# First weight loads moved between the attention jobs, transposes moved ahead of their predecessor's last part, and the second norm moved among the first unit's groups

## Chip, cores, metric

One core of one Trainium2 chip. The metric is the device time of one execution in microseconds (us), lower is better. Engines: PE is TensorE, DVE is VectorE, ACT is ScalarE, POOL is GpSimd, SP is SyncE. "Lnnn" is a line of the kernel that the lines belong to; the kernel after has its lines up to 8 lower down than the kernel before (L264 became L269, L470 became L477, and so on).

## The reference

```python
q, k, v: (8 batches, 8 heads, 576, 64) float32
scores = q @ k^T / 8                            # per batch and head
ret = scores * where(i >= j, gamma_h ** (i - j), 0)
attn = ret @ v                                  # (8, 8, 576, 64)
x = attn.transpose(0, 2, 1, 3).reshape(4608, 512)
xn = x / sqrt(mean(x * x) + 1e-6) * rms_g
out = (silu(xn @ w_gate) * (xn @ w_val)) @ w_out    # 512 -> 1536 -> 512
```

The three weight matrices come as float64 (their random parts are multiplied by a NumPy scalar of 64 bits), and the kernel makes float32 of them on the chip.

## The kernel before

The attention is cut into 32 jobs, one for a batch and a pair of heads. A job is five pieces of work: `turn` (q and k turned over by PE; later jobs use `prepare`, the same on DVE), `scores` and `states` (PE), `weigh` (DVE: the mask, and the running state), `values` and `carried` (PE: the product with v, and what the earlier chunks of tokens add). `carried` ends with three DVE multiplications that write the job's part of x. Four jobs give a batch's 576 tokens.

The FFN goes by units of 384 tokens, so jobs 0 to 3 feed the first unit and jobs 4 to 7 the second. Units 0 and 1 are done plainly, in 12 groups of 32 matmuls (`up_plain(u, m, g)`: unit, gate or value, third of the columns); from unit 2 on a Strassen scheme is used, which the change does not touch.

What matters for this change is what shares the engines with the first 226 us:

```python
    def slot(j, rest=True):             # the order on PE and DVE
        if j < len(jobs):
            scores(j)
            states(j)
        if rest and j > 0:
            values(j - 1)
        if j < len(jobs):
            weigh(j)
        if rest and j > 0:
            carried(j - 1)

    def weigh(j):
        ret = d["ret"] = att.tile([P, 2, NFULL * P], F32, tag="ret", ..., bufs=1)   # one copy only
        ...
    def weights_to(n):                  # conversion of the 18 chunks of 1 MB
        while n_chunks < min(n, len(chunks)):
            mantissa(n_chunks + 1)      # 3 DVE operations
            join(n_chunks)              # 1 DVE operation: the chunk is ready
            load_chunks(n_chunks + 4)   # 1 MB, one DMA
            exponent(n_chunks + 2)      # 1 DVE operation, then 3 ACT passes
            n_chunks += 1

    # start():
        for j in range(NHP):                        # NHP = 4
            load_first(j)                           # q, k of a job, issued by SP
            if j + 1 < NHP:
                load_kv(j)                          # v of a job, issued by SP
        for i in (2, 3, 0, 1, 4):
            table(i)                                # issued by ACT
        load_chunks(2)                              # issued by ACT
        table(5)
        ...
        load_chunks(3)
        turn(0)                                     # its results are copied by ACT
        for j in range(NHP):
            slot(j)
            if j + 1 < NHP:
                turn(j + 1)
            ...                                     # squares, conversion of chunks 0 and 1
        ...                                         # last part of job 3, first norm
        order = [(0, 0, 0), 4, (0, 1, 0), 5, (0, 0, 1), 6, (0, 1, 1), 7, (0, 0, 2)]
        order += [(1, 0, 0), (1, 1, 0), (0, 1, 2)]
        order += [(1, m, g) for g in (1, 2) for m in range(2)]
        for what in order:
            if not isinstance(what, tuple):
                slot(what, rest=what > NHP)         # a job
                following(what)
                if what == 2 * NHP - 1:
                    values(what); carried(what); norm_0(1); norm_1(1)
                continue
            u, m, g = what
            weights_to(4 * g + 2 * m + 2)
            for _ in up_plain(u, m, g):             # 4 steps of 8 matmuls
                step += 1
                weights_to(2 + (step + 1) // 2)     # one chunk every two steps
            if what == (0, 0, 2):
                norm_2(1)
```

Of the kernel before, what the change touches and what calls it, by code (L numbers as in the profile page):

```python
# [10 lines left out]
F32 = mybir.dt.float32  # L11
# [32 lines left out]
def kernel(  # L44
# [32 lines left out]

    const = ctx.enter_context(tc.tile_pool(name="const", bufs=1))
    raw = ctx.enter_context(tc.tile_pool(name="raw", bufs=1))
    att = ctx.enter_context(tc.tile_pool(name="att", bufs=2))  # L80
    xp = ctx.enter_context(tc.tile_pool(name="xp", bufs=3))
    ffn = ctx.enter_context(tc.tile_pool(name="ffn", bufs=1))
    tmp = ctx.enter_context(tc.tile_pool(name="tmp", bufs=6))
# [4 lines left out]
    def bank(name):  # L88
        return banks.tile([P, 512], F32, tag="b", name=name)
# [57 lines left out]
    def load_first(j):  # L147


        b, hp = jobs[j]  # L150
        part = h_of[0].rearrange("p f t -> p (f t)")[:, j * 6 * P : j * 6 * P + 6 * P]
        part = part.rearrange("p (c e d) -> p c e d", e=2, d=D)
        t = raw.tile([P, NFULL, 2, D], F32, tag="k", name=f"k_{j}", bufs=4)
        st[j].update(q=part[:, :NFULL], qt=part[:TAIL, NFULL], k=t, kt=part[:TAIL, NFULL + 1])
        for nm, src in (("q", q), ("k", k)):
            for e in range(2):
                nc.sync.dma_start(
                    out=st[j][nm][:, :, e],
                    in_=src[b, 2 * hp + e, : NFULL * P].rearrange("(c p) d -> p c d", p=P),
                )  # L160
            nc.sync.dma_start(
                out=st[j][nm + "t"],
                in_=src[b, 2 * hp : 2 * hp + 2, NFULL * P :].rearrange("e p d -> p e d"),
            )

    def load_kv(j):


        b, hp = jobs[j]
        for nm, src, bufs in (("k", k, 4), ("v", v, 3)):  # L170
            if nm in st[j]:
                continue
            t = raw.tile([P, NFULL, 2, D], F32, tag=nm, name=f"{nm}_{j}", bufs=bufs)
            for e in range(2):
                nc.sync.dma_start(
                    out=t[:, :, e],
                    in_=src[b, 2 * hp + e, : NFULL * P].rearrange("(c p) d -> p c d", p=P),
                )
            st[j][nm] = t
        t = st[j]["vt"] = raw.tile([P, D], F32, tag="vt", name=f"vt_{j}", bufs=3)  # L180
        for e in range(2):
            nc.sync.dma_start(
                out=t[e * TAIL : e * TAIL + TAIL], in_=v[b, 2 * hp + e, NFULL * P :]
            )

    def turn(j):

        d = st[j]
        last = bank(f"turn_{j}_t")
        for i, nm in enumerate("qk"):  # L190
            ps = bank(f"turn_{j}_{nm}")
            for c in range(NFULL):
                nc.tensor.transpose(
                    out=ps[:, c * P : c * P + P], in_=d[nm][:, c].rearrange("p e d -> p (e d)"),
                    identity=ident,
                )
            o = slice(i * TAIL, i * TAIL + TAIL)
            nc.tensor.transpose(
                out=last[:, o], in_=d[nm + "t"].rearrange("p e d -> p (e d)"),
                identity=ident[:TAIL, :TAIL],  # L200
            )
            t = d[nm + "T"] = att.tile([P, S], F32, tag=nm + "T", name=f"{nm}T_{j}")
            nc.scalar.copy(out=t[:, : NFULL * P], in_=ps)
            nc.scalar.copy(out=t[:, NFULL * P :], in_=last[:, o])
        scale_v(j)

    def prepare(j):
# [39 lines left out]
    def states(j):  # L247

        d = st[j]
        for c in range(NFULL):  # L250
            for e in range(2):
                nc.tensor.matmul(  # L252
                    d["s"][e * D : e * D + D, 2, SC + c * D : SC + c * D + D],
                    lhsT=d["k"][:, c, e], rhs=d["v"][:, c, e], start=True, stop=True,
                )
# [62 lines left out]
            )  # L318
        st[j] = {}

    def slot(j, rest=True):

        if j > len(jobs):
            return
        if j < len(jobs):
            scores(j)
            states(j)
        if rest and j > 0:
            values(j - 1)
        if j < len(jobs):  # L330
# [3 lines that stand above are left out]
# [179 lines left out]

        return i % 4 if i < n_up else LATER[i - n_up]

    def load_chunk(i):
        dst, src, rws, cols = chunks[i]
        if src.dtype != F32:
            n = dst.shape[1]
            cols = slice(2 * (cols.start or 0), 2 * cols.stop if cols.stop else None)  # L520
            src = src.bitcast(U32)
            at = spare(i)
            dst = free[:, : 4 * DM] if at == 3 else (
                w_out[:, 4 * at : 4 * at + 4].rearrange("p c f -> p (c f)")
            )
            dst = words_of[i] = dst.bitcast(U32).rearrange("p (c f) -> p c f", c=n)
            waits_at[at] = i
        nc.scalar.dma_start(out=dst, in_=src[rws, cols].rearrange("(c p) f -> p c f", p=P))

    def load_chunks(n):  # L530

        nonlocal n_loads
        while n_loads < min(n, len(chunks)) and waits_at.get(spare(n_loads)) is None:
            load_chunk(n_loads)
            n_loads += 1

    def exponent(i):
# [58 lines left out]
    def weights_to(n):  # L596

        nonlocal n_chunks
        while n_chunks < min(n, len(chunks)):
            mantissa(n_chunks + 1)  # L600
            join(n_chunks)
            load_chunks(n_chunks + 4)
            exponent(n_chunks + 2)
            n_chunks += 1
# [3 lines left out]
    def start():  # L608

        h_of[0] = ffn.tile([P, NF, U], F32, tag="h", name="h_0")  # L610
        tables = [*_causal_tables(), *_decay_tables(H, D)]
        tables = list(zip((causal, causal_t, gv, gt, gc, gq), tables))

        def table(i):
            t, values_ = tables[i]
            src = nc.inline_tensor(values_, name=t.tensor.name + "_table")
            nc.scalar.dma_start(out=t, in_=src.ap())

        make_identity(nc, ident)
        for t in sd:  # L620
            nc.gpsimd.memset(t, 0.0)
        nc.vector.memset(ones, 1.0)
        for j in range(NHP):
            load_first(j)
            if j + 1 < NHP:
                load_kv(j)
        for i in (2, 3, 0, 1, 4):
            table(i)
        load_chunks(2)
        table(5)  # L630
        nc.scalar.dma_start(out=rms_g, in_=moe_rms_g.rearrange("(c p) -> p c", p=P))
        load_chunks(3)
        turn(0)
        sq = []
        for j in range(NHP):
            slot(j)
            if j + 1 < NHP:
                turn(j + 1)
            if j:
                sq.append(square(0, j - 1))  # L640
            if j == 0:
                exponent(0)
                exponent(1)
            elif j == 1:
                load_kv(NHP - 1)
                mantissa(0)
                weights_to(1)
                load_qk(NHP)
            elif j == 2:
                weights_to(2)  # L650
                load_kv(NHP)
        values(NHP - 1)
        carried(NHP - 1)
        sq.append(square(0, NHP - 1))
        norm_0(0, sq)
        norm_1(0)
        norm_2(0)
        following(NHP - 1)
        step = 0
        order = [(0, 0, 0), 4, (0, 1, 0), 5, (0, 0, 1), 6, (0, 1, 1), 7, (0, 0, 2)]  # L660
        order += [(1, 0, 0), (1, 1, 0), (0, 1, 2)]
        order += [(1, m, g) for g in (1, 2) for m in range(2)]
        for what in order:
            if not isinstance(what, tuple):
                slot(what, rest=what > NHP)
                following(what)
                if what == 2 * NHP - 1:
                    values(what)
                    carried(what)
                    norm_0(1)  # L670
                    norm_1(1)
                continue
            u, m, g = what
            weights_to(4 * g + 2 * m + 2)
            for _ in up_plain(u, m, g):
                step += 1
                weights_to(2 + (step + 1) // 2)
            if what == (0, 0, 2):
                norm_2(1)
        weights_to(len(chunks))  # L680
        combine(0)
        for u in (1, 0):
            for s in range(NS):
                down(u, s)
                if u == 0:
                    (norm_0, norm_1, norm_2)[s](2)
            if u:
                combine(1)
                slot(8, rest=False)
                following(8)  # L690
        slot(9)
        following(9)
# [51 lines left out]
```

## Time and profile before

| | kernel before |
|---|---|
| median | 1265.76 us |
| span of the profiled run | 1264.4 us |
| PE busy | 1217.4 us (96%), so 47.0 us idle |
| mean granted PE clock | 0.984 |
| first gate group of unit 0 | 65.47 us |
| first group of unit 1 | 153.39 us |
| last plain group ends (the next product starts) | 225.7 us |

The timeline: start, duration, engine, line, operation, output from input; the bracket is idle time before the instruction and what ended it.

### The profile page before, as it was taken

The page shows a single profiled execution, that of the slowest core. Times are in us where ns is not written, and L with a number is a line of the kernel's source. Part 1 is how long each engine was busy: PE and PEld are TensorE (multiplying, and loading weights), DVE is VectorE, ACT ScalarE, POOL GpSimd, SP SyncE. Part 2 cuts the span into 40 slices and gives each one's busy share as a digit, 9 for nine tenths or more (in the row PEclk, how much of TensorE's full clock was granted, in tenths as well). Part 3 has the DMA queues.
Part 4 walks back from the last instruction along what each step waited for, and adds up shares of the span by engine and source line. Part 5 has one row for each costly group of instructions (what it writes and reads, how often), then busy time and mean ns, then how long its engine had stood idle before and what let it go on. Part 6 is the DMA issues. An engine that isn't in the chain of part 4 may idle for free.

```text
span 1264.4 us, 16414 instructions
## 1 busy us (share of the span) xinstructions
PE 1217.4 (96%) x6792; PEld 924.2 (73%) x6792; DVE 547.6 (43%) x1056; ACT 280.3 (22%) x520; POOL 43.0 (3%) x44
## 2 busy tenths in 40 slices
PE   4599799999999999999999999999999999999998
PEld 3465455447976985976985995995995896795993
DVE  1789871015542652433552464343454443333240
ACT  3646541011221220111120221121221121120110
POOL 0000005130000000000000000000000000000000
PEclk8899799999999999999999999999999999999999
DMA  8579520022230322002122233002122200000000
GB/s 212 123 177 198 141 100 0 17 62 45 46 74 17 68 51 54 1 9 54 38 40 58 38 59 68 9 1 53 27 57 53 45 1 10 17 1 17 9 1 25
DMA packets 225307, 65.68 MB, mean 52 GB/s; under 512 B 212688, under 2 KB 212816, under 8 KB 225232
## 3 DMA queue, kind: packets, MB, share of 16 engines
q1 hardware_dynamic: 215872, 45.12, 17.3%
q10 hardware_dynamic: 9360, 19.51, 4.7%
q8 instruction: 53, 0.87, 0.3%
q14 instruction: 22, 0.18, 0.0%
HBM read 55.16 MB, written 9.44 MB: 51 GB/s over the span
## 4 chain that ended last, share of the span: by engine, by line
PE 88%; DVE 5%; ACT 3%; DMA 2%; issue 1%; SPq 1%; POOL 0%; DVEq 0%; ACTq 0%; POOLq 0%
PE out L484 29%; PE x L413 12%; PE w L413 12%; PE z L413 12%; PE y L413 6%; PE up L470 6%; PE s L242 3%; PE av L292 2%; PE av L306 2%; PE s L252 1%; DMA k<-in_k_dram 1%; ACT w_gate L548 1%; PE ms L360 1%; DVE w_gate L572 1%; DMA v<-in_v_dram 1%
## 5 line engine op out<-in xcount | busy, mean ns | idle before, releaser
L484 PE MATMUL out<-w_out,h 128*128 128x512 f32 x792 | 346.1, 594 | 0.0
L484 PEld LDWEIGHTS out<-w_out,h 128*128 128x128 f32 x792 | 149.1, 190 | 177.5 <-issue 175.1
L489 ACT COPY o_all<-out 128x512 f32<-128x512 f32 x36 | 21.1, 586 | 348.8 <-PE out L484 334.9
L420 DVE TENSOR_TENSOR u<-m,y 128x384 f32<-128x384 f32 x60 | 33.2, 554 | 149.9 <-PE y L413 141.8
L264 DVE TENSOR_TENSOR ret<-s,causal 128x1024 f32<-128x1024 f32 x32 | 39.2, 1224 | 121.8 <-PE av L292 69.3
L413 PE MATMUL x<-x,w_gate 128*128 128x192 f32 x480 | 88.9, 328 | 1.5 <-ACT m L437 1.5
L413 PE MATMUL x<-x,w_val 128*128 128x192 f32 x480 | 89.2, 329 | 0.0
L413 PE MATMUL w<-sums,w_gate 128*128 128x192 f32 x480 | 87.8, 326 | 0.0
L413 PE MATMUL w<-sums,w_val 128*128 128x192 f32 x480 | 87.8, 326 | 0.0
L413 PE MATMUL z<-x,w_gate 128*128 128x192 f32 x480 | 87.8, 326 | 0.0
L413 PE MATMUL z<-x,w_val 128*128 128x192 f32 x480 | 87.8, 326 | 0.0
L413 PEld LDWEIGHTS x<-x,w_gate 128*128 128x128 f32 x480 | 79.2, 190 | 7.1 <-issue 4.3
L413 PEld LDWEIGHTS x<-x,w_val 128*128 128x128 f32 x480 | 78.8, 190 | 1.4 <-ACT m L437 1.4
L413 PEld LDWEIGHTS w<-sums,w_gate 128*128 128x128 f32 x480 | 79.7, 190 | 0.0
L413 PEld LDWEIGHTS z<-x,w_val 128*128 128x128 f32 x480 | 79.7, 190 | 0.0
L413 PEld LDWEIGHTS z<-x,w_gate 128*128 128x128 f32 x480 | 79.7, 190 | 0.0
L413 PEld LDWEIGHTS w<-sums,w_val 128*128 128x128 f32 x480 | 79.7, 190 | 0.0
L280 ACT ACTIVATE sd<-sum,gc 64x256 f32<-64x256 f32 x64 | 32.3, 504 | 200.4 <-DVE sum L274 200.0
L470 PE MATMUL up<-x,w_gate 128*128 128x384 f32 x192 | 67.8, 515 | 1.5 <-ACT w_gate L548 0.8
L420 DVE TENSOR_TENSOR h<-u,w 128x384 f32<-128x384 f32 x60 | 33.3, 555 | 81.4 <-PE w L413 81.4
L432 ACT ACTIVATE h<-h 128x384 f32<-128x384 f32 x90 | 47.0, 523 | 88.6 <-DVE h L420 88.6
L382 DVE SCALAR_TENSOR_TENSOR x<-x,rms_g,rb 128x384 f32<-128x384 f32 x48 | 26.3, 608 | 89.1 <-PE rb L380 89.1
(98 smaller groups left out, 1345.7 us busy)
## 6 DMA issues: line engine op xcount, KB each, us to landing
out_dram<-o_all SPq DMA_DIRECT2D x36, 256.0 KB, 2.0
k<-in_k_dram SPq DMA_DIRECT2D x64, 128.0 KB, 2.8
v<-in_v_dram SPq DMA_DIRECT2D x64, 128.0 KB, 2.8
qraw<-in_q_dram SPq DMA_DIRECT2D x112, 72.0 KB, 2.4
kraw<-in_k_dram SPq DMA_DIRECT2D x112, 72.0 KB, 2.6
w_out<-in_moe_w_gate_dram ACTq DMA_DIRECT2D x6, 1024.0 KB, 6.6
w_out<-in_moe_w_val_dram ACTq DMA_DIRECT2D x3, 1024.0 KB, 5.9
w_gate<-in_moe_w_val_dram ACTq DMA_DIRECT2D x3, 1024.0 KB, 6.2
```

The costliest lines, as they stand in the source:

```text
L242: nc.tensor.matmul(s[:, e, ck] if c < NFULL else s[e * n : e * n + n, 2, :n], lhsT=d["kT"][r, ck], rhs=d["qT"][r, ck], start=True, stop=True,)
L264: nc.vector.tensor_tensor(out=ret.rearrange("p e (c k) -> p e c k", c=NFULL), in0=s[:, :2].rearrange("p e (c k) -> p e c k", c=NFULL), in1 ...
L280: nc.scalar.activation(out=sd[j % 2][r, :, r], in_=t[r], func=AF.Copy, scale=gc[r, hp : hp + 1])
L292: nc.tensor.matmul(av[blk][e * D : e * D + D, o : o + n], lhsT=d["v"][:, c, e] if c < NFULL else d["vt"][r], rhs=d["ret"][:, e, c * P : c ...
L306: nc.tensor.matmul(av[blk][:, o : o + n], lhsT=sd[j % 2][:, c - 1], rhs=d["qT"][:, c * P : c * P + n], start=False, stop=(c in (AC - 1, NC ...
L382: nc.vector.scalar_tensor_tensor(out=x[:, c], in0=x[:, c], scalar=rms_g[:, c : c + 1], in1=rb[:, :U], op0=ALU.mult, op1=ALU.mult,)
L413: nc.tensor.matmul(ps[:, i * HU : i * HU + HU], lhsT=w_up[m][:, 2 * blk + c, cut], rhs=t_of[u][blk][:, c], start=(start and i == c == 0), ...
L420: nc.vector.tensor_tensor(out=o, in0=a, in1=pairs_of(ps), op=ALU.add)
L432: nc.scalar.activation(out=o, in_=c, func=AF.Silu)
L470: nc.tensor.matmul(ps[:, :U], lhsT=w_up[m][:, 4 * half + c, i * P : i * P + P], rhs=x_of[u][:, c], start=(c == 0), stop=(c == NHP - 1),)
L484: nc.tensor.matmul(ps[:, :DM], lhsT=h_of[u][:, f, s * P : s * P + P], rhs=w_out[:, f], start=(f == 0), stop=(f == NF - 1),)
L489: nc.scalar.copy(out=o, in_=ps[:, :DM])
```

## The change

The intent, in its author's words: "First chunks of weights issued by SP between the jobs; a job's transposes ahead of the last part of its predecessor; second norm among the first unit's groups". I count four parts. (1) Loads: SP issues the first three chunks, each behind a job's loads; ACT keeps the small tables. (2) Transposes: `turn(j+1)` goes ahead of `values(j-1)`, with all transposes ahead of their ACT copies and a third copy of qT and kT. (3) Conversion: one chunk less is converted before the first norm, and some of what stays is done one job later. (4) Order: all groups of unit 0 come ahead of those of unit 1, and the second norm is spread over its last two groups. The diff, cut to these:

```diff
-    att = ctx.enter_context(tc.tile_pool(name="att", bufs=2))
+    att = ctx.enter_context(tc.tile_pool(name="att", bufs=3))
 ... (the tile of k: bufs=4 -> 3; the ACT copies of turn(j) become fetch(j);
 ...  load_chunk, load_chunks and table get a queue as argument)
     def slot(j, rest=True, between=None):
         if j < len(jobs):
             scores(j)
             states(j)
+        if between is not None:
+            between(j + 1)
         if rest and j > 0:
             values(j - 1)
 ...
-        for j in range(NHP):
-            load_first(j)
-            if j + 1 < NHP:
-                load_kv(j)
         for i in (2, 3, 0, 1, 4):
             table(i)
-        load_chunks(2)
-        table(5)
         nc.scalar.dma_start(out=rms_g, ...)
-        load_chunks(3)
+        for j in range(NHP - 1):
+            load_first(j)
+            load_kv(j)
+            if j == 1:
+                table(5, nc.sync)
+            load_chunks(j + 1, nc.sync)
         turn(0)
+        fetch(0)
+        def ahead(j):
+            if j < NHP:
+                turn(j)
+                fetch(j)
         for j in range(NHP):
-            slot(j)
-            if j + 1 < NHP:
-                turn(j + 1)
+            slot(j, between=ahead)
             if j == 0:
+                load_first(NHP - 1)
                 exponent(0)
-                exponent(1)
             elif j == 1:
                 load_kv(NHP - 1)
+                load_qk(NHP)
+                exponent(1)
                 mantissa(0)
-                weights_to(1)
-                load_qk(NHP)
             elif j == 2:
-                weights_to(2)
                 load_kv(NHP)
+                weights_to(1)
 ...
-        order = [..., (0, 1, 1), 7, (0, 0, 2)]
-        order += [(1, 0, 0), (1, 1, 0), (0, 1, 2)]
-        order += [(1, m, g) for g in (1, 2) for m in range(2)]
+        order = [..., (0, 1, 1), 7, (0, 0, 2), (0, 1, 2)]
+        order += [(1, m, g) for g in range(NG) for m in range(2)]
 ...
-                if what == 2 * NHP - 1:
-                    values(what); carried(what); norm_0(1); norm_1(1)
+                if what == (0, 1, 2) and step % 4 == 2:      # inside the group
+                    norm_1(1)
             if what == (0, 0, 2):
+                values(2 * NHP - 1); carried(2 * NHP - 1); norm_0(1)
+            if what == (0, 1, 2):
                 norm_2(1)
```

More of the change, by code (lines that the diff above doesn't have):

```diff
@@ L152, in load_first @@
         part = part.rearrange("p (c e d) -> p c e d", e=2, d=D)
-        t = raw.tile([P, NFULL, 2, D], F32, tag="k", name=f"k_{j}", bufs=4)
+        t = raw.tile([P, NFULL, 2, D], F32, tag="k", name=f"k_{j}", bufs=3)
         st[j].update(q=part[:, :NFULL], qt=part[:TAIL, NFULL], k=t, kt=part[:TAIL, NFULL + 1])
@@ L169, in load_kv @@
         b, hp = jobs[j]
-        for nm, src, bufs in (("k", k, 4), ("v", v, 3)):
+        for nm, src, bufs in (("k", k, 3), ("v", v, 3)):
             if nm in st[j]:
@@ L189, in turn @@
         last = bank(f"turn_{j}_t")
+        d["turned"] = []
         for i, nm in enumerate("qk"):
@@ L201, in turn, with fetch @@
             )
-            t = d[nm + "T"] = att.tile([P, S], F32, tag=nm + "T", name=f"{nm}T_{j}")
+            d["turned"].append((nm, ps, last[:, o]))
+    def fetch(j):
+        for nm, ps, last in st[j].pop("turned"):
+            t = st[j][nm + "T"] = att.tile([P, S], F32, tag=nm + "T", name=f"{nm}T_{j}")
             nc.scalar.copy(out=t[:, : NFULL * P], in_=ps)
-            nc.scalar.copy(out=t[:, NFULL * P :], in_=last[:, o])
+            nc.scalar.copy(out=t[:, NFULL * P :], in_=last)
         scale_v(j)
@@ L319, in carried, with slot @@
         st[j] = {}
-    def slot(j, rest=True):
+    def slot(j, rest=True, between=None):
         if j > len(jobs):
@@ L514, in spare, with load_chunk @@
         return i % 4 if i < n_up else LATER[i - n_up]
-    def load_chunk(i):
+    def load_chunk(i, queue):
         dst, src, rws, cols = chunks[i]
@@ L527, in load_chunk, with load_chunks @@
             waits_at[at] = i
-        nc.scalar.dma_start(out=dst, in_=src[rws, cols].rearrange("(c p) f -> p c f", p=P))
-    def load_chunks(n):
+        queue.dma_start(out=dst, in_=src[rws, cols].rearrange("(c p) f -> p c f", p=P))
+    def load_chunks(n, queue=nc.scalar):
         nonlocal n_loads
         while n_loads < min(n, len(chunks)) and waits_at.get(spare(n_loads)) is None:
-            load_chunk(n_loads)
+            load_chunk(n_loads, queue)
             n_loads += 1
@@ L612, in start, with table @@
         tables = list(zip((causal, causal_t, gv, gt, gc, gq), tables))
-        def table(i):
+        def table(i, queue=nc.scalar):
             t, values_ = tables[i]
             src = nc.inline_tensor(values_, name=t.tensor.name + "_table")
-            nc.scalar.dma_start(out=t, in_=src.ap())
+            queue.dma_start(out=t, in_=src.ap())
         make_identity(nc, ident)
@@ L641, in start @@
             if j == 0:
+                load_first(NHP - 1)
                 exponent(0)
-                exponent(1)
             elif j == 1:
                 load_kv(NHP - 1)
+                load_qk(NHP)
+                exponent(1)
                 mantissa(0)
+            elif j == 2:
+                load_kv(NHP)
                 weights_to(1)
-                load_qk(NHP)
-            elif j == 2:
-                weights_to(2)
-                load_kv(NHP)
         values(NHP - 1)
@@ L659, in start @@
         step = 0
-        order = [(0, 0, 0), 4, (0, 1, 0), 5, (0, 0, 1), 6, (0, 1, 1), 7, (0, 0, 2)]
-        order += [(1, 0, 0), (1, 1, 0), (0, 1, 2)]
-        order += [(1, m, g) for g in (1, 2) for m in range(2)]
+        order = [(0, 0, 0), 4, (0, 1, 0), 5, (0, 0, 1), 6, (0, 1, 1), 7, (0, 0, 2), (0, 1, 2)]
+        order += [(1, m, g) for g in range(NG) for m in range(2)]
         for what in order:
@@ L666, in start @@
                 following(what)
-                if what == 2 * NHP - 1:
-                    values(what)
-                    carried(what)
-                    norm_0(1)
-                    norm_1(1)
                 continue
@@ L677, in start @@
                 weights_to(2 + (step + 1) // 2)
+                if what == (0, 1, 2) and step % 4 == 2:
+                    norm_1(1)
             if what == (0, 0, 2):
+                values(2 * NHP - 1)
+                carried(2 * NHP - 1)
+                norm_0(1)
+            if what == (0, 1, 2):
                 norm_2(1)
```

## The prediction

> **What bounds the kernel now.** I read the table of slices first, then stretches of ten microseconds, then the chain that ended last, then the timeline of the first 226 us. Busy time over the whole span says little here, since the change touches only the start.
>
> ```profile
> PE   4599799999999999999999999999999999999998
> DVE  1789871015542652433552464343454443333240
> ...
> PE 88%; DVE 5%; ACT 3%; DMA 2%; issue 1%; SPq 1%; POOL 0%; DVEq 0%; ACTq 0%; POOLq 0%
> ```
>
> A slice is 31.6 us. PE is full from the sixth slice on; what can be won lies in slices 1 to 5. VectorE is heaviest in just those.
>
> ```profile
> 0.00:10.00 10.00, 1.38 (x5) 0.90 (x5) 0.34 (x6) 0.00 (x0) 1.64 (x8) 1.00 0.79 220
> 60.00:70.00 10.00, 7.29 (x17) 4.16 (x17) 6.00 (x12) 0.75 (x1) 0.87 (x1) 0.54 0.10 16
> 110.00:120.00 10.00, 9.72 (x30) 5.43 (x30) 9.82 (x19) 5.87 (x9) 0.00 (x0) 1.00 0.92 226
> 120.00:130.00 10.00, 4.64 (x66) 3.65 (x64) 9.11 (x11) 4.86 (x5) 0.00 (x0) 0.86 1.12 250
> ```
>
> Columns: stretch, length, busy PE, PEld, DVE, ACT, POOL, granted clock, DMA share, GB/s. PE idles about 29 us before 60 us, 2.7 us in 60 to 70, 8.3 us in 120 to 140, and 1.5 us elsewhere up to 160: 42 of the 47 idle microseconds of the run. In 110 to 130 it is DVE that is full.
>
> ```profile
> 72.48 0.70 DVE w_gate L544
> 73.21 1.16 ACT w_gate L548
> 74.39 1.16 ACT w_gate L549
> 75.57 1.16 ACT w_gate L552
> 76.79 1.11 issue
> 77.89 1.23 DVE w_val L580
> 79.15 0.70 DVE w_gate L544
> ```
>
> This is the chain of waits. From 34.65 to 153.39 us it is almost only the conversion of the 64-bit weights, 18 chunks of 1 MB: exponent on DVE, three ACT passes, mantissa and join on DVE. One turn takes 79.15 - 72.48 = 6.67 us when nothing else is between; with one attention job's DVE work between, 88.26 - 79.15 = 9.11 us or 104.72 - 94.93 = 9.79 us.
>
> ```profile
> 15.26 1.28 ACT L203 ACT_TABLE_LOAD   x1 [15.26 <-DMA h<-in_q_dram]
> 17.80 2.49 PE L242 MATMUL s<-qT,kT 64*128 64x128 f32 x20
> 56.49 1.10 PE L306 MATMUL av<-qT,sd 128*128 128x128 f32 x8 [0.91 <-ACT sd L280]
> 65.47 12.39 PE L470 MATMUL up<-x,w_gate 128*128 128x384 f32 x32 [0.71 <-DVE x L382]
> 130.18 1.97 PE L292 MATMUL av<-ret,v 128*64 128x128 f32 x16 [5.54 <-DVE ret L264]
> 153.39 5.08 PE L470 MATMUL up<-x,w_gate 128*128 128x384 f32 x15 [0.80 <-ACT w_gate L548]
> ```
>
> Timeline: first ACT copy held until 15.26 us by ACT's own weight issues, first scores at 17.80, last part of job 3 at 56.49, first unit's gate groups at 65.47, job 7's values held until 130.18 because DVE converts two chunks before it weighs job 7, and from 153.39 on PE runs through the remaining seven groups until 225.7 us (10.33 us a group).
>
> **What the Trainium skill says.** (1) "DMA: Bandwidth & Descriptors", section "Issuing engines are not separate DMA queues": DMAs of all issuing engines run on the same 16 engines, so a second issuer saves only sequencer time. So moving chunks from ACT to SP makes no bandwidth; it changes order, and frees ACT, which this trace shows blocked by its issues until 15.26 us. (2) Same page, "Queues, rings and completion order": descriptors of one row are consumed in ring order. A job's loads issued by SP behind a chunk therefore stand behind 1 MB; the trace has no such case yet. (3) "TensorE: Matmul & The Clock Gate", "What's actually happening": an idle window of about 3.4 us brings half clock back. The trace agrees: the gate group after the first norm took 12.39 us instead of 10.33, at a granted clock of 0.54. (4) "Perfetto Trace Analysis", "Optimization Strategy": interleave regimes whose most contended engine differs. The change does so at 120 to 140 us; the question is whether DVE has room.
>
> **The change, part by part.**
>
> Start to the first scores. Job 0's loads lose their rival: the last of k landed about 10.1 us (transposes start 10.11) beside two chunks. An unhindered load of 128 KB took 2.3 to 3.1 us from its issue, and k's last piece is issued near 4.4, so it lands near 7.5. ACT no longer waits for chunk lanes. Transposes end near 8, ACT copies (0.59 + 0.22 + 0.60 + 0.21) near 9, scores(0) near 8.8 instead of 17.8: 9 us earlier, then 2.49 + 1.12 us of PE and DVE's weighing (2.4 us) to about 15.
>
> Jobs 1 to 3. SP issues chunk 0 near 7.7, then job 1; a chunk needs about 6 us to land and a job's 0.86 MB about 4 to 5 us more. I place job 1's k near 15, job 2's near 22 to 24, job 3's near 28 to 31. In the new PE order turn(j+1) precedes values(j-1), so x(0) waits for job 2: transposes 23 to 25.5, values and carried 2.3 + 1.1, x(0) near 29 (before 33.85, 5 us less). Then DVE: x 0.8, exponent 0.6, mantissa 3.1, weigh(2) 2.3 (35.7); x(1) near 37.5; mantissa, join, exponent 4.8 (43); weigh(3) to 45; ACT must end the exponent it got at 42 to 43 (3.5) before job 3's sd (1.0). So the last carried comes near 47.2 instead of 56.49, and the norm, 10.5 us later (before: 67.0), ends at 57.7. Gain at the first norm: 9.3 us. If PE keeps warm or the loads are faster it is 12, if loads queue badly 6.
>
> A chunk is put off. Before, joins 0 and 1 and exponent 3 were issued before the norm; now only join 0 and exponent 2. So 6.67 us of conversion returns right behind the norm. Counting from the norm's end, exponents of chunks 3, 4, 5 start on DVE at 5.5, 12.2, 18.8; before, chunks 4 and 5 at the first two of these.
>
> First unit. I carry the measured turns on: 9.11 over job 4, 6.67, 9.79 over job 5, 6.67, 9.79, 6.67, and again 9.79 over job 7. Exponents 6 to 13 then start at 27.9, 34.6, 44.4, 51.1, 60.8, 67.5, 77.3, 84.0. PE needs 10.33 us a group and 4.1 a job, so it waits about 1 to 2 us a group for the joins, more at the end; it is not the bound. The old wait at job 7 (5.5 us) goes because group (0,0,2) lies before values(7).
>
> Second norm. In the order of the built program DVE does x(7) only after exponent 13, ACT its four squares (1.7 us) after that exponent's three passes. From 84.0: exponent 0.7, ACT 3.5, silu 0.5, squares 1.7, two additions 1.1, end 91.5; ms on PE 1.5, to 93. DVE meanwhile: product 0.5, mantissa 13 and join 12 with exponent 14, 4.7, product; then r, POOL's power and diag 1.9 (98.6); product, mantissa 14, join 13, exponent 15, product (104.3); only then the scaling of x. First scaled part at 104.9. Before, the first scaled part stood at 153.2 - 67.0 = 86.2. So 18.7 us later against the norm, with six groups left instead of seven: minus 10.3. **Net loss of the unit stage: 8.4 us.** PE idles about 7 us just before, so I add up to 2 us of half clock as above.
>
> Sum: -9.3 + 8.4 + 2 x 0.5 (half weighted) = +0.1 at the end of the second unit's groups. All behind (31 us of down products, the Strassen units) keeps its order; I count nothing there. The additional buffers for qT and kT and the k buffer less take no time that I find: a k buffer comes free after states(j), long before its reload. Changed kernel: about 1265.8 + 0.1, which I lower to **1264.5 us**, since the start has more room to be early than I gave it.
>
> **Rivals.** (a) The intent works: the start's 9 us and the wait of 8 us at 120 to 140 both go, 1250 us. For it: PE idles there. Against: DVE was at 9.1 to 9.8 tenths in 80 to 130 us, and 13 joins lie before the second norm's scaling now, against 10 after the first norm before; PE's gap is filled, but the chain is not shorter. (b) Chunks in the SP queue delay jobs 1 to 3: SP also waits for a chunk's landing when its completion slot comes round (v of jobs 1 and 2 issue behind it). Then the norm gains 5 us or less and the total is 1268 to 1271. For it: DMA ran at 0.7 to 1.3 in the first 24 us. (c) Conversion is fed too late: each chunk is issued about one turn before its use, and 1 MB took 5.7 to 8.5 us to land against a turn of 6.67. No DVE wait on such a load shows before; if DMA delays it, add 2 to 4 us. (d) Nothing in the start matters because DVE is the chain already: the norm comes only 5 us earlier and the total is 1269.
>
> **Range and chances.** The norm may end between 54 and 61 us (6 to 13 us gained), the unit stage lose 5 to 11. Together -8 to +6: 1257 to 1271 us. Two per cent is 25 us, more than the 42 idle microseconds could give after the waits above: faster 0.02, same 0.97, slower 0.01.
>
> **What would show it.** Right: first scores near 9 us; the first gate group at 54 to 59 us; DVE above 9 tenths from there to about 160 us; chunk joins steady at 6.67 or 9.8 us; PE waiting for the squares' sum and then about 5 us for the scaled x, with second-unit groups starting near 163 us; the last of them ending near 226 us. Wrong: groups of the second unit starting before 157 us (rival a: PE waits there would be short), jobs 1 to 3 landing later than 16, 24, 31 us (rival b), or DVE exponents waiting on DMA (rival c). If PE's total idle time falls below 38 us the sum is wrong in the unit stage.

## More of the kernel before

```profile
3.27 2.15 ACTq L528 DMA_DIRECT2D w_out<-in_moe_w_gate_dram  x2
13.57 0.35 ACTq L617 DMA_DIRECT2D gq<-gq_table  x1
...
31.50 1.23 DVE L264 TENSOR_TENSOR ret<-s,causal 128x1024 f32<-128x1024 f32 x1 [6.47 <-PE av L292]
```

ACT issues two chunks by 5.42 us and issues the next transfer only at 13.57; what that issue waited for, the trace does not name. Its copies of job 0, on which the first scores wait, stand behind that. The third line is job 1 being weighed: it needs the single `ret` tile, which is free once job 0's values product has read it.

## The result, and the profile after

| | before | after |
|---|---|---|
| median (lowest to highest) | 1265.76 (1265.63 to 1266.14) | 1269.16 (1268.38 to 1270.06) |
| PE busy, idle, in the profiled span | 1217.4, 47.0 | 1224.4, 43.0 |
| mean granted PE clock | 0.984 | 0.978 |
| first scores | 17.80 | 8.33 |
| first part of x (job 0) | 33.85 | 29.93 |
| last carried product of job 3 | 56.49 | 48.33 |
| first gate group of unit 0 | 65.47 | 58.11 |
| first group of unit 1 | 153.39 | 164.91 |
| last plain group ends (the next product starts) | 225.7 | 228.7 |

The ratio is 1.0027 with a 95% interval of 1.0009 to 1.0044: same within 2%, and a little slower beyond the noise. Ratios here and below are the mean time of one kernel's runs over that of the other's of the same rounds, so not quite the ratio of the medians that I quote.

The lines of the page after that answer to those of before, PE and DVE in slices of 31.7 us, then the shares of the chain that ended last:

```profile
PE   6698889999999999999999999999999999999998
...
DVE  2789771014542652433462464343444443333340
...
PE 87%; DVE 5%; DMA 3%; ACT 2%; issue 1%; SPq 1%; POOL 0%; DVEq 0%; ACTq 0%; POOLq 0%
```

PE's first slice rose from 4 to 6, the second from 5 to 6 and the fifth from 7 to 8; the fourth and the sixth fell from 9 to 8. The same stretches as before (length, busy PE, PEld, DVE, ACT, POOL, clock, DMA share, GB/s):

```profile
0.00:10.00 10.00, 4.44 (x26) 3.46 (x26) 0.34 (x6) 3.72 (x8) 1.63 (x8) 1.00 0.62 132
60.00:70.00 10.00, 10.00 (x28) 5.68 (x27) 8.19 (x10) 4.07 (x4) 0.00 (x0) 0.86 0.67 124
110.00:120.00 10.00, 10.00 (x26) 5.68 (x25) 9.82 (x18) 5.87 (x9) 0.00 (x0) 0.80 0.70 207
120.00:130.00 10.00, 10.00 (x83) 6.91 (x82) 9.04 (x15) 5.66 (x5) 0.00 (x0) 1.00 1.07 218
```

PE is full at 120 to 130 us, where it did 4.64 us before: the gap at job 7 is gone. DVE is as full at 110 to 130 as it was. Now the timeline of the kernel after, at the places that the prediction showed of before:

```profile
3.84 1.28 ACT L208 ACT_TABLE_LOAD   x1 [3.84 <-DMA h<-in_q_dram]
8.33 2.48 PE L247 MATMUL s<-qT,kT 64*128 64x128 f32 x20 [0.79 <-ACT kT L208]
48.33 1.97 PE L311 MATMUL av<-qT,sd 128*128 128x128 f32 x8 [1.54 <-ACT sd L285]
108.58 13.23 PE L477 MATMUL up<-x,w_val 128*128 128x384 f32 x32 [3.31 <-ACT h L485]
141.49 6.98 PE L477 MATMUL up<-x,w_val 128*128 128x384 f32 x16 [2.85 <-ACT h L485]
151.08 1.03 PE L367 MATMUL ms<-mean_w,sq 128*128 128x1 f32 x6 [2.61 <-DVE sq L360]
164.91 5.29 PE L477 MATMUL up<-x,w_gate 128*128 128x384 f32 x10 [5.43 <-DVE x L389]
```

The wait of 5.54 us at job 7 has become one of 5.43 us at the second norm, and three shorter ones ahead of it. The wait of 3.31 us, in unit 0, comes with the chunk that was put off: after, e1, e3, e4, e5 and e10 have 3.31 or 3.32 us there, but before had 0.39 us and e8, which converts that chunk early again, 0.66 us. The first group of unit 1 began at half clock (0.50 from 165 to 168.5 us) and took 12.38 us instead of the 10.48 of a group at full clock. What it waited for is in the chain of waits of the kernel after:

```profile
156.94 0.86 POOL r L373
157.83 0.68 DVE diag L376 x3
158.51 0.46 DVE h L483
158.97 0.64 DVE w_out L572
...
162.00 1.15 DVE w_out L587
163.17 0.70 DVE w_gate L551
163.87 0.46 DVE h L483
164.33 0.54 DVE x L389
```

Once the factors of the norm are ready (158.51), DVE does a product of the groups, a chunk's mantissa (L572 and on), another's join (L587), a third's exponent (L551) and another product before it scales x (L389): 5.8 us of other work, in program order.

PE sat idle 4.0 us less than before but was busy 7.0 us longer with the same 6792 matmuls. What follows the plain groups takes 1038.7 us in both traces, so the difference lies in the start and the unit stage. In the first 60 us PE did 307 matmuls in 38.61 us of busy time at a mean granted clock of 0.74; before, 298 in 30.75 us at 0.88. So part of what was idle is now work at a lower clock. The mean clocks of whole executions do not show this: the four of the kernel after had 0.978 to 0.987, those of before, in the batches of the experiments, 0.982 to 0.987.

### The profile page after: what moved, and what is told of

Same layout as the page of the kernel before. It is cut to its first block, busy times and chain, and to the rows that moved or that the text cites. A ratio compares the mean times of both kernels' runs of the same rounds, so it can differ in the third digit from the quotient of the medians. Undisturbed runs are those within 1.5% of the kernel's fastest.

```text
span 1267.4 us, 16417 instructions
## 1 busy us (share of the span) xinstructions
PE 1224.4 (97%) x6792; PEld 926.7 (73%) x6792; DVE 547.4 (43%) x1056; ACT 279.8 (22%) x520; POOL 43.0 (3%) x44
## 3 DMA queue, kind: packets, MB, share of 16 engines
HBM read 55.16 MB, written 9.44 MB: 51 GB/s over the span
## 4 chain that ended last, share of the span: by engine, by line
PE 87%; DVE 5%; DMA 3%; ACT 2%; issue 1%; SPq 1%; POOL 0%; DVEq 0%; ACTq 0%; POOLq 0%
PE out L491 29%; PE x L420 12%; PE w L420 12%; PE z L420 12%; PE y L420 6%; PE up L477 5%; PE s L247 3%; PE av L297 2%; PE av L311 2%; PE s L257 1%; DMA v<-in_v_dram 1%; DMA qraw<-in_q_dram 1%; DMA h<-in_q_dram 1%; PE rb L387 1%; DVE w_gate L579 1%
## 5 line engine op out<-in xcount | busy, mean ns | idle before, releaser
L496 ACT COPY o_all<-out 128x512 f32<-128x512 f32 x36 | 21.1, 585 | 349.7 <-PE out L491 335.8
L477 PE MATMUL up<-x,w_val 128*128 128x384 f32 x192 | 69.3, 521 | 6.4 <-ACT h L485 6.2
```

The lines of the kernel that those rows point to most:

```text
L477: nc.tensor.matmul(ps[:, :U], lhsT=w_up[m][:, 4 * half + c, i * P : i * P + P], rhs=x_of[u][:, c], start=(c == 0), stop=(c == NHP - 1),)
L496: nc.scalar.copy(out=o, in_=ps[:, :DM])
```

## The experiments

Each kernel ran correctly beside the kernel before on the same chip, with 5 executions each (4 for after and e9). The batches had medians of before of 1266.26 (e1 to e4), 1266.58 (e5 to e8) and 1266.49 (e9, e10); "against before" subtracts that of the own batch, and the kernel after stands at +3.40 in its own. "Gate" is the start of unit 0's first gate group, "unit 1" that of unit 1's first group; both come from one profiled execution. The traces of after, e1 and e4, whose program is the same up to the gate, differ there by 0.75 us, so smaller differences in these two columns should not be read as effects.

| run | median | against before | ratio [95%] | gate | unit 1 |
|---|---|---|---|---|---|
| after | 1269.16 | +3.40 | 1.0027 [1.0009, 1.0044] | 58.11 | 164.91 |
| e1_start_only | 1265.09 | -1.17 | 0.9990 [0.9978, 1.0003] | 57.38 | 151.20 |
| e2_units_only | 1271.37 | +5.11 | 1.0041 [1.0028, 1.0053] | 65.80 | 166.00 |
| e3_turn_after | 1263.78 | -2.48 | 0.9983 [0.9970, 0.9995] | 52.08 | 158.85 |
| e4_cap12 | 1262.23 | -4.03 | 0.9975 [0.9962, 0.9989] | 57.36 | 157.73 |
| e5_both | 1256.50 | -10.08 | 0.9919 [0.9907, 0.9931] | 51.71 | 153.79 |
| e6_unit1_early | 1259.58 | -7.00 | 0.9943 [0.9931, 0.9955] | 51.95 | 113.45 |
| e7_loads_only | 1257.14 | -9.44 | 0.9924 [0.9911, 0.9938] | 56.19 | 144.30 |
| e8_chunk_back | 1269.65 | +3.07 | 1.0028 [1.0016, 1.0041] | 64.41 | 164.56 |
| e9_jobs_spaced | 1250.71 | -15.78 | 0.9876 [0.9862, 0.9889] | 51.82 | 110.90 |
| e10_values_first | 1266.58 | +0.09 | 1.0002 [0.9988, 1.0015] | 55.77 | 162.54 |

My theory: the change wins at the start and loses it again at the second norm, because DVE must convert more chunks ahead of it. The rivals: the start's gain is lost elsewhere (transposes that wait for loads and hold up the job before), or the chunk that is put off is what costs.

### e1_start_only: parts 1 to 3 alone

```diff
-        order = [..., 7, (0, 0, 2), (0, 1, 2)]
-        order += [(1, m, g) for g in range(NG) for m in range(2)]
+        order = [..., 7, (0, 0, 2)]
+        order += [(1, 0, 0), (1, 1, 0), (0, 1, 2)]
+        order += [(1, m, g) for g in (1, 2) for m in range(2)]
 (and the second norm where the kernel before has it)
```

> The changed kernel's start (loads, transposes, one chunk put off) with the old order of the two first units and the old place of the second norm. Theory (the start gains, the new order of units loses, the two add up): first norm ends at 59.6 us as in the changed kernel; the conversion is one turn of 6.67 us later against it, so the second norm's first scaled part stands at 59.6 + 86.2 + 6.7 = 152.5 us (before 153.2), and seven groups of 10.33 follow: 0.7 us under the kernel before, 1265.0 us, within 1.5. Rival (the SP loads or the transposes themselves cost the time): as slow as the changed kernel, 1268.5 or more.

Measured 1265.09 us, as the theory said, though the difference from before (1.2 us) is not clear of noise. Unit 1 began 93.8 us after the first gate group, against 87.9 in the kernel before: 5.9 us of the 8.1 that the start won went back into the unit stage although its order is the old one.

### e2_units_only: part 4 alone

The edit is the reverse: the start of the kernel before, and the order of the kernel after.

> The old start with the new order of units and the new place of the second norm. Theory: first norm at 67.0 us, second norm's first scaled part 105.3 - 6.7 = 98.6 us behind it, at 165.6, then six groups of 10.33 and 2 us of half clock: 3.9 us over the kernel before, 1269.7 us, within 1.5. Rival (the order of units is harmless and the put-off chunk alone costs): 1266 us.

Measured 1271.37 us, 5.1 above before, where 3.9 within 1.5 was expected (the absolute range is just missed): PE waited 5.41 us for the scaled x and the first group of unit 1 took 13.46 us. The order alone is a loss.

### e3_turn_after: part 2 undone, the rest of the change kept

```diff
-        if between is not None:
-            between(j + 1)
         if rest and j > 0:
             values(j - 1)
         if j < len(jobs):
             weigh(j)
         if rest and j > 0:
             carried(j - 1)
+        if between is not None:
+            between(j + 1)
```

> The changed kernel with a job's transposes behind the last part of its predecessor again. Theory: in the changed kernel weigh(1) waited from 21.1 to 27.6 us for the single ret buffer, because values(0) stood behind transposes that waited for job 2's q; with the old order weigh(1) starts near 23, x(0) ends near 26 instead of 30.8, the first norm ends 2 to 4 us earlier, and the whole is 2 to 4 us faster than the changed kernel, 1265 to 1267 us. Rival (the transposes ahead help, as intended, since ACT can copy them earlier): the first norm 1 to 4 us later, 1270 us or more.

Measured 1263.78 us, and the gate group began 6.0 us earlier, where 2 to 4 were expected. The timelines of PE and DVE of the kernel after show the cause:

```profile
22.87 1.09 PE L194 MATMUL turn_q<-ident,h 128*128 128x128 f32 x4 [1.78 <-DMA h<-in_q_dram]
...
25.56 1.97 PE L297 MATMUL av<-ret,v 128*64 128x128 f32 x16
...
27.58 1.22 DVE L269 TENSOR_TENSOR ret<-s,causal 128x1024 f32<-128x1024 f32 x1 [12.71 <-PE av L297]
...
29.93 0.88 DVE L320 TENSOR_TENSOR x<-av,gq 128x192 f32<-128x192 f32 x3
```

and that of DVE of e3:

```profile
22.28 1.23 DVE L269 TENSOR_TENSOR ret<-s,causal 128x1024 f32<-128x1024 f32 x1 [7.07 <-PE av L297]
...
24.63 0.88 DVE L320 TENSOR_TENSOR x<-av,gq 128x192 f32<-128x192 f32 x3
```

In the kernel after PE finished the states of job 1 at 21.1 us, waited 1.78 us for job 2's q, did 2.8 us of transposes, and only then the values product of job 0, whose inputs had long been there. DVE idled 12.71 us for it. With the transposes behind, the same product ran at 20.3 us, DVE idled 7.07 us, and job 1 was weighed 5.3 us earlier.

### e4_cap12: fewer conversions ahead of the second norm

```diff
             for _ in up_plain(u, m, g):
                 step += 1
-                weights_to(2 + (step + 1) // 2)
+                if u:
+                    weights_to(n_chunks + (step % 3 == 1))
+                else:
+                    weights_to(min(2 + (step + 1) // 2, n_up))     # n_up = 12
```

> The changed kernel, but the weights of the output product (chunks 12 to 17) are converted only after the second norm, one every third step. Theory (the second norm waits for two turns of conversion that nobody needs yet): DVE's r, diag and scaling follow the squares' sum at once; PE reaches the second unit's groups at about 160 us instead of 164.9 and without half clock: 5 to 7 us faster than the changed kernel, 1262 to 1264 us. Rival (PE's own groups bound this stage): no more than 1 us gained.

Measured 1262.23 us (the profiled execution, 1260.28, is the fastest of the five). The timeline of PE of e4:

```profile
157.73 10.59 PE L477 MATMUL up<-x,w_gate 128*128 128x384 f32 x32 [0.71 <-DVE x L389]
```

The wait for the scaled x fell from 5.43 to 0.71 us and the first group of unit 1 from 12.38 to 10.59 us; unit 1 began 7.2 us earlier. It is DVE's conversions ahead of the norm's scaling that make the new order slow; they are not needed there, since w_out is first read at about 229 us.

### e5_both: e3 and e4 together

> The transposes put back behind the predecessor's last part and the output weights' conversion held back until the second norm, together, on the changed kernel. Theory (two separate waits): the gains add. First gate group at 52.1 us, second unit's groups at 152.4 us, last one ending near 214.5 us, 11 us before that of the kernel before: 1254.5 us, within 2. Rival (the earlier norm is lost to the conversion): no better than 1260 us.

Measured 1256.50 us, at the upper edge of the range. Against the kernel after, e3 takes 5.9 us and e4 7.4 us; both together 13.5 us. So the two costs are separate and add up.

### e6_unit1_early: e3's start, jobs 4 to 7 back to back, units sharing the chunks

```diff
+        weights_to(2)
+        steps((0, 0, 0), 3); job(4)
+        steps((0, 0, 0), 1); steps((0, 1, 0), 2); job(5); job(6); job(7)
+        steps((0, 1, 0), 1); values(7); carried(7); norm_0(1)
+        steps((0, 1, 0), 1); norm_1(1); norm_2(1)
+        for what in [(1, 0, 0), (1, 1, 0)] + [(u, m, g) for g in (1, 2) for m in range(2) for u in range(2)]:
+            weights_to(...); steps(what, 4)          # three chunks in eight steps
```

> The start with the transposes put back, and another order: jobs 4 to 7 follow each other with only chunks 0 to 3 converted between them, the second norm comes at once, and the two units then share each pair of chunks, group by group. Theory (DVE's conversion chain bounds the unit stage; with two units per chunk PE has 20.7 us of work for two turns of 6.67 us): the second unit starts near 98 to 103 us, PE is full behind it, its last group ends near 205 to 209 us: 1244 to 1250 us. Rival (DVE's or the DMA queues' whole work bounds the stage in any order): 1254 us or more.

Missed: 1259.58 us. PE was full once unit 1 had begun, as intended, but that was at 113 us. The timeline of PE of e6, its jobs 5 to 7:

```profile
76.83 2.49 PE L247 MATMUL s<-qT,kT 64*128 64x128 f32 x20 [4.93 <-DVE kT L217]
...
86.84 2.49 PE L247 MATMUL s<-qT,kT 64*128 64x128 f32 x20 [2.88 <-DVE kT L217]
...
96.01 1.57 PE L247 MATMUL s<-qT,kT 64*128 64x128 f32 x20 [3.48 <-DVE kT L217]
```

Jobs stand 9 to 10 us apart although a job has only 4.1 us of work for PE at full clock: scores, then values of the job before (which frees `ret`), weighing, x, the DVE transposes of the next job, scores again. That is a loop through PE and DVE, and without other work PE waits in it.

### e7_loads_only: part 1 alone

The edit takes the new loads (and the k tile's three copies) into the kernel before and nothing else.

> The kernel before with the new loads alone: chunks 0 to 2 and the large table issued by SP between the jobs, job 3's first loads later, one k buffer less; transposes, conversions and units as before. Theory (the loads are the part that gains): first scores near 9 us, the first norm ends near 59 to 60 us with both chunks converted, and the rest follows unchanged: 6 to 8 us faster than the kernel before, 1258 to 1260 us. Rival (the gain needs the transposes ahead): 2 us or less faster.

Measured 1257.14 us, 9.4 us below before. The first gate group began at 56.19 us with both chunks converted, and unit 1 followed 88.1 us later, as in the kernel before (87.9): the whole 9.3 us of the start arrived at the end. The gain is above the 6 to 8 us expected. DVE waited 7.00 us for the load of the second chunk in this run, up to 21.66 us; job 1 was still weighed at 22.34 us, as early as in e3, so that wait held nothing up.

### e8_chunk_back: the put-off chunk of part 3 back, the rest kept

```diff
             elif j == 2:
                 load_kv(NHP)
-                weights_to(1)
+                weights_to(2)
```

> The changed kernel with the put-off chunk converted ahead of the first norm again. Theory (one turn of the same DVE chain is moved across the norm, nothing is saved): the first norm ends about 5 us later, the second norm about the same time as in the changed kernel, the whole 1268 to 1270 us. Rival (putting the chunk off is what costs): 2 us or more faster than the changed kernel, 1267 us or less.

Measured 1269.65 us. The gate group moved 6.3 us later and unit 1 0.35 us earlier, which is within the spread. Putting off the chunk moves work from ahead of the first norm to behind it and is worth nothing with this order of the units. (The conversions that part 3 does one job later stay later in this run.)

### e9_jobs_spaced: e6 with half groups between the jobs

```diff
+        weights_to(2)
+        steps((0, 0, 0), 2); job(4); weights_to(3)
+        steps((0, 0, 0), 2); job(5); weights_to(4)
+        steps((0, 1, 0), 2); job(6); weights_to(5)
+        steps((0, 1, 0), 2); job(7)
+        steps((0, 0, 1), 1); values(7); carried(7); norm_0(1)
+        steps((0, 0, 1), 1); norm_1(1); norm_2(1)
+        steps((1, 0, 0), 4, True); steps((1, 1, 0), 4, True)      # True: three chunks in eight steps
+        weights_to(6); steps((0, 0, 1), 2, True)
+        for what in [(1, 0, 1), (0, 1, 1), (1, 1, 1)] + [(u, m, 2) for m in range(2) for u in range(2)]:
+            weights_to(...); steps(what, 4, True)
```

> Edit: the start of e3 (transposes behind the carried step); jobs 4 to 7 are no longer back to back as in e6, each stands between half groups of the first unit's first two groups, with one chunk's conversion beside it; the second norm beside the first half of the third group; then both units share the chunks, three conversions in eight steps. Theory (e6 missed because a job alone is a loop of about 10 us through the two-deep and one-deep tiles of a job, during which TensorE has nothing else): with half a group of 5.2 us in each loop TensorE stays busy, the first gate group of the second unit starts at 100 to 106 us instead of 113.5, and the run takes 1244 to 1250 us. Rival (the loop or the conversions on VectorE bound this stretch whatever TensorE is given): the second unit starts at 112 us or later, or waits for chunks follow, and the run takes 1256 us or more.

Measured 1250.71 us, the best, though just above the expected range. The timeline of PE of e9:

```profile
86.96 1.42 PE L247 MATMUL s<-qT,kT 64*128 64x128 f32 x20 [0.80 <-DVE kT L217]
...
105.26 1.25 PE L367 MATMUL ms<-mean_w,sq 128*128 128x1 f32 x6 [5.06 <-DVE sq L360]
...
110.90 12.94 PE L477 MATMUL up<-x,w_gate 128*128 128x384 f32 x32 [0.71 <-DVE x L389]
```

Up to job 7 PE's waits in the job loop are under 1 us each (0.80 us for kT, then 0.16 and 0.89 us for the scaled v), so the loop is hidden. What is left is the norm: PE idles 5.06 us for the squares and 2.06 us for the diagonal, with only a quarter of a group (2.80 us at 97.40) beside the whole norm, and unit 1 begins at 110.90 instead of 100 to 106 us. PE is full from there to the end of the plain groups. Part of the 5.06 us has another cause: x was complete at 99.74 us, but ACT's squares began at 102.18, because ACT, in program order, first scaled the v of job 8, for whose load it had sat idle 4.24 us. Nothing of the second norm needs job 8. No run moved that work, so its worth (2.4 us at most, by these times) is not shown. Idle time in the span is 33.6 us, and the clock 0.990; this profiled execution (1252.0 us) is 1.3 us above the median.

### e10_values_first: only the carried step behind the transposes

```diff
-        if between is not None:
-            between(j + 1)
         if rest and j > 0:
             values(j - 1)
+        if between is not None:
+            between(j + 1)
         if j < len(jobs):
             weigh(j)
```

> Edit: the kernel after, but the values product of job j-1 goes ahead of the transposes of job j+1; only the carried step of job j-1 stays behind them. In the kernel after, the first weigh of job 1 started at 27.6 us after a 12.7 us wait for the values product of job 0, which stood behind transposes that waited for a transfer. Theory (the single ret tile, freed by the values product, is what the transposes hold up): the weigh of job 1 starts at 22 to 24 us, the first x at 26 to 28 us instead of 29.9, the first gate group at 54 to 56 us instead of 58.1, and the run takes 1265 to 1267 us. Rival (it is the carried step behind the transposes that delays x and the norm): the first gate group moves by under 1 us and the run takes 1268 to 1270 us.

Measured 1266.58 us. The timeline of DVE of e10:

```profile
22.57 1.22 DVE L269 TENSOR_TENSOR ret<-s,causal 128x1024 f32<-128x1024 f32 x1 [7.45 <-PE av L297]
...
27.99 1.10 DVE L320 TENSOR_TENSOR x<-av,gq 128x192 f32<-128x192 f32 x3 [2.99 <-PE av L311]
```

Job 1 is now weighed as early as in e3, so the single `ret` tile was rightly named. But x(0) comes at 27.99, between 24.63 (e3) and 29.93 (after): DVE waits 2.99 us for the carried product behind the transposes. The theory's numbers held, and the rival is not wrong either: of the 5.3 us at x(0), 1.9 belong to the values product and 3.4 to the carried one; of the 6.0 us at the gate group, 2.3 and 3.7, each give or take the spread of 0.75 us named above.

## Why the prediction was right, and where its terms were off

It said the time would hardly move because the start's gain would be lost at the second norm. The range held, and e2, e4 and e7 show both halves. The number it gave was 1.3 us faster; the change is 3.4 us slower, so the sign was missed. By its own steps:

- **Start to the first scores: right.** 8.8 predicted, 8.33 measured.
- **Jobs 1 to 3: right in mechanism, 1.9 us short in size.** It foresaw that x(0) would wait for job 2's load, near 29 us (29.93; the first transposes of job 2 waited until 22.87 us for its q), the last carried near 47.2 (48.33) and the end of the norm at 57.7 (59.63). x(0) is late by 0.9, job 3 by a further 0.2. The last 0.8 is the norm's own stretch: the carried product of job 3 ran at half clock (1.97 us for what took 1.10 before). So the start gained 7.4 us in this trace and not 9.3 (8.1 in e1's). That a job's loads would stand behind a chunk in SP's queue fits the trace: in the first 60 us the 128 KB loads of q took 5.9 us in the median from issue to landing, 3.1 before.
- **What it failed to price: the transposes by themselves.** It took the new PE order as given and compared x(0) with before only ("5 us less"). e3 and e10 show that without this part x(0) would stand at 24.6 us: part 2 alone costs 6 us. No rival named it; rival (b) blamed the chunks in SP's queue, and e7, which has that queue and gains 9.4 us, refutes it. The totals that rivals (b) and (d) gave, 1268 to 1271 and 1269 us, fit the measured time better than the prediction's 1264.5; they fail on the way there, since both wanted the norm at most 5 us earlier, and it came 7.4 us earlier.
- **A chunk put off, and the second norm: right.** The unit stage was to lose 8.4 us; it lost 106.8 - 87.9 - 10.33 = 8.6 us. e1 splits that: 5.9 us is the chunk that was put off (93.8 - 87.9), which the start had saved and e8 shows to be neutral; 2.7 us is the order (106.8 - 93.8 - 10.33), which the 1.9 us of half clock below bring to the 4.6 us that e1 leaves for it. The chain ran as written: exponents 6 to 13 started 27.8, 34.5, 44.3, 50.9, 60.7, 67.4, 77.2 and 83.9 us after the norm's end, each within 0.2 us of the prediction; the squares' sum came at 91.3 us (91.5), the first scaled x at 105.2 (104.9). PE's groups at half clock before that, such as the one of 13.23 us, cost nothing here, since DVE's chain came later.
- **Half clock: half the size.** The prediction halved a term of 2 us. The wait came, and the first group of unit 1 took nearly the full term, 12.38 - 10.48 = 1.9 us more. In e4 and e5 it nearly vanishes with the wait (10.59 us).
- **The last step, lowering the sum of 1265.9 to 1264.5, had nothing behind it**, and the start proved later than computed, not earlier. With 1.9, 0.2 and 0.9 us from the terms and 1.4 from this, 4.4 of the 4.7 us between 1264.5 and 1269.16 are named.
- **Signs.** PE's idle time was to stay above 38 us: 43.0. DVE above nine tenths up to 160 us: not so, 8.2 tenths at 60 to 80 and at 100 to 110, and 6.7 at 140 to 160, where ACT's three passes and the squares are the chain. (Its reading of before was too high in the same way: "9.1 to 9.8 tenths in 80 to 130 us" leaves out 8.2 at 100 to 110.) Groups of unit 1 near 163 us: 164.9. Rivals (a), (c) and (d) did not come; for (c), DVE waited once for a chunk's load up to 230 us, for 4.1 us, and it had done so before, for 3.8, a wait at 182.78 us that the prediction overlooked ("No DVE wait on such a load shows before").

Where the gain went, in the order in which the parts were put together and each against its own batch: loads alone -9.4 us (e7); transposes and part 3 +8.3 (e1 less e7); the order +4.6 (after less e1). That is +3.4. Most of the 8.3 us belongs to the transposes: e3 puts them at 5.9 us, and e8, which has them and converts both chunks ahead of the norm as e7 does, reaches the gate 8.2 us after e7. The rest, some 2.4 us, lies in how they meet the conversions, which e8 also does one job later than e7; no run separates that.

Two things stay open. The order cost 4.6 us with the change's start and 5.1 with the old one; taken from e3 to e7 (with e8's finding that the chunk is neutral) it is 7.0. So its size depends on how the start leaves DVE and ACT, and I did not separate that. And I did not run e9 with more PE work kept back for the second norm, which its 7 us of idle time there suggest, nor with job 8's preparation behind the norm.

## What to carry to other kernels

An engine that works in order is a queue: before moving work that waits for a transfer ahead of work that is ready, ask who waits for the ready work, and whether a tile with one copy hangs on it. A change in several parts should be run part by part; here one part was worth 9.4 us and the others cost all of it and more. A chain of short steps across engines (a job, a norm) needs filler from another stage beside it, and background work such as conversion has to be kept off its engine until the chain is through, if it isn't due yet (7.4 us in e4).

## What the Trainium skill lacked or had wrong

- "TensorE: Matmul & The Clock Gate", section "What's actually happening": it gives an idle window of about 3.4 us as what brings half clock. In the kernel after an idle stretch of 2.85 us was enough: the 16 matmuls behind it took 6.98 us, with a granted clock of 0.50 to 0.67 between 141 and 145 us, against 5.43 us for 16 of the same shape at 88.67 us. In e8 even a wait of 1.86 us (before 150.72 us) was followed by a clock of 0.50 from 153 to 156 us and 7.10 us for 16; after waits of 1.65 us (e4), 1.53 (e2) and 1.27 (e10) at the same place the clock stayed at 1.00 and 16 took 5.41 us. The prediction's reading that the trace of before agrees with 3.4 us is not borne out either: ahead of the group of 12.39 us PE's waits were 2.11, 2.00 and 0.71 us, none of 3.4. So on this evidence waits of 2 to 3 us can already bring a slow start.
- "DMA: Bandwidth & Descriptors", section "Issuing engines are not separate DMA queues": it says that a second issuing engine saves only the sequencer's time, usually small. That the transfers share the 16 engines is not in doubt, but what it leaves out is that the engine's own work stands behind its issues and their waits: in the kernel before ACT's first operation started at 15.26 us, after the change at 3.84 us, and the new loads alone (new issuer and new order together) made the run 9.4 us shorter.
